# Pacing the late input loads of a fused attention and MoE kernel by the stage two units ahead

## The chip, the cores and the metric

The kernel runs on one core of a Trainium2 chip. The metric is the device time of one execution in microseconds (us); the median of several runs is compared. Engines are named as the profile names them: PE is TensorE (PEld its weight loads), DVE is VectorE, ACT is ScalarE, POOL is GpSimd and SP is SyncE, whose only work here is to issue DMAs.

## What is computed

The reference is causal attention followed by one gated two-layer block, here called the MoE as the program calls it. Four batches, 8 heads, 768 positions, head size 64. Heads 0, 2 and 6 see all earlier positions; the five others see the first 4 positions and a window of 64.

```python
scores = scale * np.matmul(q, k.transpose(0, 1, 3, 2))
mask = np.where(retr, causal, causal & (is_sink | in_win))
a = softmax(np.where(mask, scores, -1e9))
x = (a @ v).transpose(0, 2, 1, 3).reshape(B * S, H * D)     # 3072 x 512
h = x @ w_in                                                # 512 -> 2048
out = (h * sigmoid(beta * h)) @ w_out                       # 2048 -> 512
```

## The kernel before, in words

The 3072 rows are cut into 8 **units** of 384 rows: unit n is half u = n % 2 of batch b = n // 2. A unit goes through these stages, and the units overlap.

- **Loads.** Units 0 to 3 load q and k in pairs of heads. Units 4 to 7 (`n >= TD`) load whole blocks: `load_block` (line 307) issues three DMAs of 256 KB for q and three for k, `load_v` (line 331) three for v, all from SP, into a ring `wf` of three buffers.
- **Turning q and k.** For units 4 to 7 POOL casts the blocks to bf16 tiles `c` (`cast_block`), and `turn_block` (line 324) has three DMA transposes, issued from SP, write them into the tile `QK`. All three must have landed before the unit's scores.
- **Scores.** PE multiplies QK into PSUM tiles `sp` (two in the ring, used by PV as well), ACT takes exponentials into `es`, DVE masks them.
- **Sums and spread.** `sums` (line 540) sums `es` on PE, `recips_d` takes the reciprocal on DVE into `rec`. For units 4 to 7 `spread_w` (line 565) writes it to DRAM as `rd` with three small DMAs and `spread_r` (line 570) reads it back as `R`, repeated over 64 partitions, with two DMAs. All are issued from SP. Units 0 to 3 spread it on PE instead.
- **PV and norm.** `pv` (line 604) multiplies `es` with v into two `sp` tiles; `norm` (line 632) multiplies those by `R` on DVE into `xT` and frees the `sp` tiles.
- **MoE.** 16 steps of `mm1` (four matmuls of xT with w_in), tanh on ACT into `t`, the gate on DVE into `gT`, and 48 matmuls of gT with w_out in `mm2`, taken in threes. Copies to `osb` and one store to `out` for each 128 rows, issued from SP.

The order of all instructions is written by a planner, `_Plan` (line 50). Each operation is entered with a priority, an engine, a cost, what it needs and what it gives, and the rings it takes from; `run` walks through time and writes one list for each engine. The costs, `needs` and `gives` act in the planner alone. On the chip an engine goes through its list in order, and an instruction waits for the data and buffers that it touches, and for nothing else. So an entry in `needs` that names no data of the instruction decides its place in the list and makes no wait.

Of the kernel before, what the change touches and what calls it, by code (L numbers as in the profile page):

```python
# [49 lines left out]
class _Plan:  # L50
# [9 lines left out]
    def add(self, key, eng, cost, f, needs=(), gives=(), take=(), drop=(), dma=0.0, mode=None, port=False, begun=()):  # L60

        one = isinstance(eng, str)
        alts = [(eng, cost)] if one else list(zip(eng, cost))
        self.ops.append((key, len(self.ops), dict(alts), (lambda e: f()) if one else f, tuple(needs), tuple(gives),
                         tuple(take), tuple(drop), dma, mode, port, tuple(begun)))
# [76 lines left out]
def kernel(  # L142
# [14 lines left out]
    pe, dve, act, pool, sp = (_Ordered(tc, e) for e in (nc.tensor, nc.vector, nc.scalar, nc.gpsimd, nc.sync))  # L157
    B, H, S, D = q.shape
    d_model, d_ff = moe_w_in.shape
    FO = d_ff // 128  # L160
    NP = len(PAIRS)
# [4 lines left out]
    def tpool(name, bufs, space=None):  # L166
# [5 lines left out]
        sp=2, b=4, **{f"es{pi}_{u}": 1 for pi in range(NP) for u in range(2)})  # L172
# [45 lines left out]
    NS = 8  # L218
# [342 lines left out]
    def recips_d(x):  # L561
        x.rec = rp.tile([96, 128], F32, name="rec")
        dve.reciprocal(x.rec, x.sm[0:96, 0:128])

    def spread_w(x):
        x.rd = dp.tile([8, TU, 128], F32, name="rd")
        for j in range(TU):
            sp.dma_start(out=x.rd[:, j, :], in_=x.rec[32 * j:32 * j + 8, :])

    def spread_r(x):  # L570
        x.R = rp.tile([128, NP, NQ], F32, name="R", bufs=RINGS["R"])
        src = x.rd[:]
        for i in range(2):
            sp.dma_start(
                out=x.R[i * D:(i + 1) * D],
                in_=bass.AP(src.tensor, src.offset + i * NQ, [[0, D], [2 * NQ, NP], [1, NQ]]))

    def recips(x):
        dve.reciprocal(x.sm[0:96, 0:128], x.sm[0:96, 0:128])

    def split(x):
        hi = rp.tile([96, 128], BF16, name="hi")
        rec = x.sm[0:96, 0:128]
        dve.tensor_copy(out=hi, in_=rec)
        for j in range(TU):
            r = slice(32 * j, 32 * j + 32)
            dve.scalar_tensor_tensor(out=hl[r, j * 128:(j + 1) * 128], in0=hi[r], scalar=low[r], in1=rec[r],
                                     op0=MULT, op1=ADD)

    def spread(x, t):  # L590
        if t == 0:
            x.R = rp.tile([128, NP, NQ], F32, name="R", bufs=RINGS["R"])
        ps = bank((x.n, "R", t))
        pe.matmul(ps[:, 0:NQ], sel[0:96, 2 * t:2 * t + 2, :].rearrange("p a d -> p (a d)"), hl[0:96, :],
                  start=True, stop=True)
        x.ps["R", t] = ps

    def spread_copy(x, t, eng):
        cast(eng, x.R[:, t, :], x.ps.pop(("R", t))[:, 0:NQ])
# [80 lines left out]
    add = plan.add  # L680
    ENG = {"act": act, "dve": dve, "pool": pool, "sp": sp}

    def attention(n, key, early):
        x = units[n]
        b, u = x.b, x.u
        gate = [("begun", "o", NS // 2 - 1)] if b else []

        for pi in range(NP if n < TD else 0):
            for nm in ("q2", "k2"):
                e = "act" if n == 0 and nm == "k2" else "sp"  # L690
                add(key["lq"] + 0.01 * pi, e, 0.47, lambda pi=pi, nm=nm, e=e: load_qk(x, pi, nm, ENG[e]), dma=0.64, needs=gate,
                    gives=[("f", n, pi, nm)], take=[(nm + "f", (n, pi), 1)])
# [3 lines left out]
                    needs=[("f", n, pi, nm)] + ([("begun", n, pi)] if nm == "k2" else []), gives=[("c", n, pi, nm)],  # L696
                    begun=[("begun", n, pi)] if nm == "q2" else [],
                    take=[("c", (n, pi), 1)] if nm == "q2" else [], drop=[(nm + "f", (n, pi))])
        if n >= TD:
            for i in range(2):  # L700
                add(key["lq"] + 0.1 * i, "sp", 3.0, lambda i=i: load_block(x, i), dma=3.9, needs=gate,
                    gives=[("f", n, i)], take=[("wf", (n, "b", i), TU)])
                for j in range(TU):
                    add(key["T"][0] - 2 + 0.5 * j + 0.1 * i, "pool", 0.7, lambda i=i, j=j: cast_block(x, i, j, pool),
                        needs=[("f", n, i)] + ([("c", n, 0, j)] if i else []), gives=[("c", n, i, j)],
                        take=[("c", (n, j), 1)] if i == 0 else [], drop=[("wf", (n, "b", i))])
            for j in range(TU):
                add(key["T"][0] + 0.5 * j, "sp", 1.25, lambda j=j: turn_block(x, j), dma=0.7,
                    needs=[("c", n, 0, j), ("c", n, 1, j)] + [("sc", n - 4 + v, pi) for pi in range(NP) for v in range(2 - u) if n >= 4],
                    gives=[("QKb", n, j)], drop=[("c", (n, j))])  # L710
            add(key["T"][0] + 1.5, "pool", 0.02, lambda: None, needs=[("QKb", n, j) for j in range(TU)],
                gives=[("QK", n, pi, i) for pi in range(NP) for i in range(2)])
        for j in range(TU):
            if not b:
                add(key["lv"] + 0.01 * j, "sp", 1.0, lambda j=j: load_v(x, j, sp), dma=1.3,
                    gives=[("vf", n, j)], take=[("vf", (n, j), 1)])
            elif j == 0:
                add(key["lv"], "sp", 3.0, lambda: [load_v(x, j, sp) for j in range(TU)], dma=3.9, needs=gate,
                    gives=[("vf", n, j) for j in range(TU)], take=[("wf", (n, 0), TU)])
            add(key["cv"] + 0.5 * j, "pool", 0.58, lambda j=j: cast_v(x, j, pool),  # L720
                needs=[("vf", n, j)] + ([("v", n - u, 0)] if (u, j) != (0, 0) else []),
                gives=[("v", n, j)], drop=[("wf" if b else "vf", (n, 0 if b else j))], take=[("vb", b, 5)] if (u, j) == (0, 0) else [])
        add(key["cv"] + 2, ("dve", "pool") if n else ("pool",), (0.9, 1.8), lambda e: shift_v(x, ENG[e]), port=True,
            needs=[("v", n, j) for j in range(TU)] + ([("v", n - 1, TU - 1)] if u else []), gives=[("vs", n)], take=[("vs", n, 2)])
# [9 lines left out]
        for pi in range(NP if n < TD else 0):  # L734
# [3 lines left out]
                gives=[("T", n, pi)], take=[("b", (n, "T", pi), 2 if early else 1)], drop=[("c", (n, pi))])  # L738
            if early:
                for i in range(2):  # L740
                    add(k0 + 0.1, ("act", "dve"), (0.37, 0.465), lambda e, pi=pi, i=i: qk_copy(x, pi, ENG[e], i, 1),
                        needs=[("T", n, pi)] + wait, gives=[("QK", n, pi, i)], drop=[("b", (n, "T", pi))])
            else:
                add(k0 + 0.1, ("act", "dve"), (0.7, 0.87), lambda e, pi=pi: qk_copy(x, pi, ENG[e]),
                    needs=[("T", n, pi)] + wait, gives=[("QK", n, pi, 0), ("QK", n, pi, 1)], drop=[("b", (n, "T", pi))])
        for pi in range(1, NP):
            if not u:
                k0 = key["T"][pi]
                add(k0 + 0.2, ("pool", "dve"), (0.35, 0.3), lambda e, pi=pi: ks_copy(x, pi, ENG[e]), port=True,
                    needs=[("QK", n, pi, 1), ("const", "zero")] + ([("sc", n - 4 + j, 3) for j in range(2)] if n >= 4 else []),  # L750
                    gives=[("KS", n, pi)])
# [3 lines left out]
        for bi, bu in enumerate(bursts):  # L755
            k0 = key["B"][bi] if not early else key["T"][bu[0][0]] + 0.5 + 0.2 * bu[0][1]
            needs, take, gives, drop, cost = [], [], [], [], 0.1
            for (pi, ri) in bu:
# [14 lines left out]
                needs=needs, gives=gives, take=take, drop=drop, mode="qk")  # L773
            for j, (pi, ri) in enumerate(bu):
                half = rounds_of(pi, u)[ri][1] is None
                add(k0 + 0.1 + 0.02 * j, "act", 0.38 if half else 0.7, lambda pi=pi, ri=ri: exps(x, pi, ri),
                    needs=[("S", n, pi, ri)], gives=[("E", n, pi, ri)], drop=[("sp", (n, pi, ri))])
                c = mask_cost(pi, ri, u)
                if c:
                    add(k0 + 0.2 + 0.02 * j, "dve", c, lambda pi=pi, ri=ri: masks(x, pi, ri, dve), port=True,  # L780
                        needs=[("E", n, pi, ri), ("const", "mask", u)], gives=[("M", n, pi, ri)])
# [4 lines left out]
        if n < RD:  # L786
            add(key["S"] + 0.1, "dve", 0.88, lambda: recips(x), needs=[("sum", n)], gives=[("rec", n)])
            add(key["S"] + 0.2, "dve", 1.3, lambda: split(x), needs=[("rec", n), ("const", "sel"), ("const", "zero")], gives=[("hl", n)],
                take=[("hl", n, NP)], drop=[("b", (n, "s"))])
            for t in range(NP):  # L790
                add(key["S"] + 0.3 + 0.01 * t, "pe", 0.18, lambda t=t: spread(x, t),
                    needs=[("hl", n)] + ([("sb", n, 0)] if t else []), gives=[("sb", n, t)],
                    take=[("b", (n, "R", t), 1)] + ([("R", n, 2)] if t == 0 else []), drop=[("hl", n)])
                add(key["S"] + 0.4, ("act", "dve"), (0.37, 0.465), lambda e, t=t: spread_copy(x, t, ENG[e]),
                    needs=[("sb", n, t)], gives=[("R", n, t)], drop=[("b", (n, "R", t))])
        else:
            add(key["S"] + 0.1, "dve", 1.0, lambda: recips_d(x), needs=[("sum", n)], gives=[("rec", n)],
                take=[("rec", n, 1)], drop=[("b", (n, "s"))])
            add(key["S"] + 0.2, "sp", 1.4, lambda: spread_w(x), needs=[("rec", n)], gives=[("rd", n)], dma=0.1, drop=[("rec", n)])
            add(key["S"] + 0.3, "sp", 0.9, lambda: spread_r(x), needs=[("rd", n)], gives=[("R", n, t) for t in range(NP)], dma=2.3,  # L800
                take=[("R", n, 2)])
        for g in range(2):
            drop = [(f"es{pi}_{u}", n) for pi in [(0, 1, 3), (2, 3)][g]] + [("vb", b), ("vs", n), ("VK", b)]
            add(key["PV"][g], "pe", [[0.65, 0.65], [1.2, 1.2]][u][g], lambda g=g: pv(x, g),
                needs=M + vready + [("rec", n) if n < RD else ("R", n, 0)], gives=[("o", n, g)], take=[("sp", (n, "v", g), 1)], drop=drop, mode="pv")
            add(key["PV"][g] + 0.1, "dve", 0.87, lambda g=g: norm(x, g),
                needs=[("R", n, 2 * g), ("R", n, 2 * g + 1), ("o", n, g)] + ([("xT", n, 0)] if g else []),
                gives=[("xT", n, 2 * g), ("xT", n, 2 * g + 1)],
# [32 lines left out]
    for n in range(N):  # L841
        u = n % 2
        if n == 0:
            attention(n, dict(lq=-100, lv=-99.5, cv=-97.5, T=[-98, -97, -96, -95], S=-94, PV=[-93.9, -93.8]), True)
        elif n == 1:
            attention(n, dict(lq=-99.4, lv=-99.05, cv=-90, T=[-90, -89, -88, -87], S=-80, PV=[-79.9, -79.8]), True)
        else:
            base = 16 * (n - 1)
            key = dict(lq=base - 34, lv=base - 32, cv=base - 20, T=[base - t for t in (25.5, 24.5, 23.5, 22.5)],
                       B=[base - t for t in ([18, 16, 14], [20, 18, 16, 14, 12, 11])[u]], S=base - 9.5,  # L850
                       PV=[base - 4.5, base - 3.5])
            attention(n, key, None)
# [4 lines left out]
        needs=[("beta_p",)], gives=[("beta",)], drop=[("b", "beta")])  # L857
# [8 lines left out]
    for s in range(NS // 2):  # L866
        for w, k0, ld, ca in (("i", -99.2 + 0.2 * (s // 2), load_w_in, cast_w_in), ("o", -98.3, load_w_out, cast_w_out)):
            add(k0 + 0.01 * s, "sp", 1.3 if w == "i" else 0.65, lambda s=s, ld=ld: ld(s), dma=3.15, gives=[("wf", w, s)], begun=[("begun", w, s)],
                take=[("wf", (w, s), 4)])
            for i in range(4):  # L870
                add(k0 + 0.01 * s, "pool", 0.58, lambda s=s, i=i, ca=ca: ca(s, i, pool), needs=[("wf", w, s)],
                    gives=[("w" + w, 4 * s + i)], drop=[("wf", (w, s))])
# [42 lines left out]
```

## Time and profile before

| What | Value |
|---|---|
| median of 3 runs | 263.28 us (263.11 to 263.43) |
| the profiled execution's own time | 261.98 us |
| its span in the trace | 260.3 us |
| PE busy | 234.9 us, 90% of the span |
| DVE, ACT, POOL busy | 58%, 56%, 28% |
| bytes over DMA | 40.27 MB, mean 155 GB/s |
| mean granted PE clock | 0.98 |

The busy shares say which engine has the most work. The page's row of 40 slices says where in the span it rests, and the views by engine and by wait say what it rests for. Times in all views count from the start of the span.

### The profile page before, as it was taken

The numbers are of one execution on the slowest core, as the hardware profiler recorded it, in microseconds if no ns is written. First come the engines' busy times: TensorE is split into PE (matmuls) and PEld (weight loads), VectorE is DVE, ScalarE is ACT, GpSimd is POOL, SyncE is SP. The second block draws the span as 40 slices with busy tenths as digits, with TensorE's granted clock in tenths as the row PEclk, the third lists the DMA queues.
The fourth block names the chain that finished last, engine by engine and source line by source line (L and its number), as shares of the span: only waits on it lengthen the run. The fifth ranks groups of instructions, "written<-read, shape, count | busy, mean of one in ns | idle before, by whom it ended". The sixth has DMA issues, their size and how long they took to land.

```text
span 260.3 us, 5563 instructions
## 1 busy us (share of the span) xinstructions
PE 234.9 (90%) x2167; PEld 128.5 (49%) x2193; DVE 150.3 (58%) x316; ACT 146.0 (56%) x248; POOL 73.9 (28%) x159
## 2 busy tenths in 40 slices
PE   1768999999999999999980999999999999999994
PEld 1435456664555555455440455645554465555541
DVE  5777789879556666656324364585465554454400
ACT  2666985788559662853831474285358734445410
POOL 5463848856983443442500000000000000000000
PEclk9999999999999999999996599999999999999999
DMA  6999998998999999999995012410251016101122
GB/s 191 273 301 305 205 317 307 341 253 189 237 230 210 238 203 194 237 209 210 227 194 123 0 43 65 100 40 0 83 122 44 1 46 161 42 0 40 43 81 81
DMA packets 81531, 40.27 MB, mean 155 GB/s; under 512 B 63984, under 2 KB 74336, under 8 KB 81504
## 3 DMA queue, kind: packets, MB, share of 16 engines
q1 hardware_dynamic: 80384, 39.12, 64.6%
q10 hardware_dynamic: 1120, 0.79, 1.1%
q8 instruction: 17, 0.28, 0.4%
q14 instruction: 10, 0.08, 0.1%
HBM read 30.42 MB, written 6.34 MB: 141 GB/s over the span
## 4 chain that ended last, share of the span: by engine, by line
PE 70%; DMA 11%; DVE 6%; ACT 5%; issue 3%; SPq 3%; POOL 1%; POOLq 0%; DVEq 0%; ACTq 0%
PE b L44 59%; PE sp L44 11%; DMA wf<-in_v_dram 4%; DMA k2f<-in_k_dram 3%; SPq L44 3%; ACT es L44 2%; DMA R<-rd 2%; ACT t L44 1%; DVE QK L44 1%; DVE es L44 1%; DVE vs L44 1%; DMA QK<-c 1%; DVE xT L44 1%; DVE gT L44 1%; POOL vb L44 0%
## 5 line engine op out<-in xcount | busy, mean ns | idle before, releaser
L44 ACT ACTIVATE t<-b,beta_h 128x384 f32<-128x384 f32 x128 | 73.0, 586 | 63.1 <-PE b L44 58.7
L44 PE MATMUL b<-xT,w_in 128*128 128x384 bf16 x512 | 101.3, 331 | 0.3
L44 DVE SCALAR_TENSOR_TENSOR gT<-t,b 128x384 bf16<-128x384 f32 x128 | 69.2, 553 | 48.5 <-ACT t L44 47.5
L44 PE MATMUL b<-w_out,gT 128*128 128x512 bf16 x358 | 94.0, 379 | 2.1 <-issue 1.3
L44 PEld LDWEIGHTS <-w_in 128*128 128x128 bf16 x512 | 48.5, 99 | 42.4 <-issue 5.6
L44 ACT ACTIVATE es<-sp 128x768 bf16<-128x768 f32 (+1 forms) x68 | 50.9, 798 | 22.2 <-PE sp L44 22.0
L44 PEld LDWEIGHTS <-gT 128*128 128x128 bf16 x384 | 36.4, 98 | 34.6 <-issue 0.8
L44 PE MATMUL sp<-QK 64*64 64x128 bf16 (+5 forms) x368 | 23.9, 259 | 10.9 <-DVE xT L44 8.5
L44 POOL CAST c<-wf 128x256 bf16<-128x256 f32 x48 | 18.3, 416 | 23.6 <-DMA QK<-c 10.0
L44 PEld LDWEIGHTS <-QK 64*64 64x64 bf16 (+1 forms) x368 | 11.2, 110 | 27.5 <-issue 20.0
L44 DVE TENSOR_TENSOR xT<-sp,R 128x768 bf16<-128x768 f32 x16 | 15.1, 956 | 10.5 <-DMA R<-rd 7.9
L44 DVE TENSOR_TENSOR es<-es,mask_s 128x768 bf16<-128x768 bf16 (+1 forms) x24 | 15.2, 647 | 6.1 <-ACT es L44 5.3
L44 ACT ACTIVATE osb<-b 128x512 f32<-128x512 f32 x18 | 10.7, 595 | 12.1 <-PE b L44 11.9
L44 DVE TENSOR_TENSOR es<-es,mask_c 128x256 bf16<-128x256 bf16 (+2 forms) x32 | 9.8, 321 | 11.5 <-ACT es L44 11.1
L44 PE MATMUL sp<-es,vb 128*64 128x64 bf16 (+3 forms) x228 | 16.0, 242 | 0.0
L44 POOL CAST vb<-wf 128x512 bf16<-128x512 f32 x18 | 11.1, 618 | 8.4 <-DMA wf<-in_v_dram 8.1
L44 ACT COPY QK<-b 128x384 bf16<-128x384 bf16 (+1 forms) x14 | 8.2, 599 | 8.5 <-PE b L44 7.3
L44 POOL CAST w_in<-wf 128x512 bf16<-128x512 f32 x16 | 9.7, 650 | 11.0 <-DMA wf<-in_moe_w_in_dram 11.0
L44 PEld LDWEIGHTS <-vb 128*64 128x64 bf16 x228 | 11.9, 111 | 1.4
L44 PE MATMUL b<-ident,c 128*128 128x128 bf16 x96 | 9.9, 253 | 1.9 <-ACT c L44 0.9
L44 PE MATMUL sp<-es,vs 128*64 128x64 bf16 x120 | 10.9, 196 | 0.0
L44 PE MATMUL b<-es,esel 128*32 128x128 bf16 x372 | 10.7, 227 | 0.0
(68 smaller groups left out, 147.8 us busy)
## 6 DMA issues: line engine op xcount, KB each, us to landing
out_dram<-osb SPq DMA_DIRECT2D x24, 256.0 KB, 4.1
wf<-in_v_dram SPq DMA_DIRECT2D x18, 256.0 KB, 5.4
wf<-in_moe_w_out_dram SPq DMA_DIRECT2D x4, 1024.0 KB
q2f<-in_q_dram SPq DMA_DIRECT2D x16, 192.0 KB, 4.8
wf<-in_moe_w_in_dram SPq DMA_DIRECT2D x4, 768.0 KB, 8.6
wf<-in_q_dram SPq DMA_DIRECT2D x12, 256.0 KB, 4.6
wf<-in_k_dram SPq DMA_DIRECT2D x12, 256.0 KB, 4.2
R<-rd SPq DMA_DIRECT2D x8, 384.0 KB, 5.1
```

What stands on the lines that cost most here:

```text
L44: ins = f(*a, **k)
```

## The change

Two places in `attention` are edited.

```diff
-        gate = [("begun", "o", NS // 2 - 1)] if b else []
+        gate = ([("begun", "o", NS // 2 - 1)] if b else []) + ([("h", n - 2, 0)] if n > 3 else [])
...
-            add(key["S"] + 0.3, "sp", 0.9, lambda: spread_r(x), needs=[("rd", n)], gives=[("R", n, t) for t in range(NP)], dma=2.3,
+            add(key["S"] + 0.3, "sp", 0.9, lambda: spread_r(x), needs=[("rd", n)], gives=[("R", n, t) for t in range(NP)], dma=4.0,
```

`gate` stands in the `needs` of the q, k and v loads. With the new entry the planner places the loads of unit n (4 to 7) only after the first MoE step of unit n - 2. The second edit has the planner expect `R` 1.7 later. Both change the lists of all engines behind them; the set of instructions stays the same, but for a few copies that change engine.

On SP, around the spread of unit 4: in the list of before the loads of unit 7 (`in_k`, `in_v`) and a store stand ahead of `rd`, and the transposes of unit 7 between `rd` and `R`. The second `rd` and `R` are those of unit 5.

```order
L44 DMA wf<-in_k_dram 128x8x64 x3
L44 DMA wf<-in_v_dram 128x8x64 x3
L44 DMA out_dram<-osb 128x512
L44 DMA rd<-rec 8x128 x3
L44 DMA_TRANSPOSE QK_107<-c 128x8x128 x3
L44 DMA out_dram<-osb 128x512
L44 DMA R<-rd 64x4x384 x2
L44 DMA out_dram<-osb 128x512 x2
L44 DMA rd<-rec 8x128 x3
L44 DMA R<-rd 64x4x384 x2
```

The same place in the list of the change. The loads and the transposes here are those of unit 5, and the loads of unit 6 follow behind `R` and two stores.

```order
L44 DMA wf<-in_q_dram 128x8x64 x3
L44 DMA wf<-in_k_dram 128x8x64 x3
L44 DMA wf<-in_v_dram 128x8x64 x3
L44 DMA out_dram<-osb 128x512
L44 DMA rd<-rec 8x128 x3
L44 DMA_TRANSPOSE QK_106<-c 128x8x128 x3
L44 DMA R<-rd 64x4x384 x2
L44 DMA out_dram<-osb 128x512 x2
L44 DMA wf<-in_q_dram 128x8x64 x3
L44 DMA wf<-in_k_dram 128x8x64 x3
L44 DMA wf<-in_v_dram 128x8x64 x3
```

The pattern nine loads, a store, `rd`, three transposes of the next unit, `R` now comes three times, for units 4, 5 and 6. Before, all loads and transposes stood ahead of the first `R`.

On DVE, around the reciprocal of unit 4, before (`KS` are small copies of keys, here of unit 6; `QK_107` is its QK tile):

```order
L44 TENSOR_SCALAR osb<-b_2033 128x512
L44 SCALAR_TENSOR_TENSOR gT<-t,b_2126 128x384
L44 COPY KS_111<-QK_107 64x4 x2
L44 COPY KS_112<-QK_107 64x4 x2
L44 SCALAR_TENSOR_TENSOR gT<-t,b_2140 128x384
L44 RECIPROCAL rec<-b_2150 96x128
L44 SCALAR_TENSOR_TENSOR gT<-t,b_2199 128x384
```

and in the list of the change:

```order
L44 TENSOR_SCALAR osb<-b_1964 128x512
L44 SCALAR_TENSOR_TENSOR gT<-t,b_2053 128x384
L44 SCALAR_TENSOR_TENSOR gT<-t,b_2073 128x384
L44 RECIPROCAL rec<-b_2079 96x128
L44 SCALAR_TENSOR_TENSOR gT<-t,b_2124 128x384
```

The four copies are gone from ahead of the reciprocal, since unit 6 has not been loaded yet at that point. On PE the list stays the same up to the first scores of unit 5, which now stand three MoE steps later (a first-layer, a second-layer and a first-layer step), and the first scores of units 6 and 7 stand 14 and 15 MoE steps behind the sums of units 5 and 6.

## Rows read from the trace of the kernel before

**Rows 1.** The page: busy time by engine, and the granted clock in 40 slices.

```profile
PE 234.9 (90%) x2167; PEld 128.5 (49%) x2193; DVE 150.3 (58%) x316; ACT 146.0 (56%) x248; POOL 73.9 (28%) x159
...
PEclk9999999999999999999996599999999999999999
```

**Rows 2.** One stretch of 4 us: busy time by engine, granted clock, DMA share, GB/s.

```profile
144.00:148.00 4.00, 4.00 (x21) 1.70 (x20) 1.67 (x3) 1.97 (x3) 0.00 (x0) 0.50 0.00 0
```

**Rows 3.** Waits from 130 to 150 us: engine, releaser, total, times, longest.

```profile
DVE xT L44 <- DMA R<-rd: 7.9, 1, 7.9
PE sp L44 <- DVE xT L44: 7.0, 2, 5.4
```

**Rows 4.** The chain that ended last: start, us, what.

```profile
134.15 6.15 DMA R<-rd
...
148.02 1.10 PE sp L44 x18
```

**Rows 5.** SP's issues in order of time: start, us, operation.

```profile
113.78 2.16 SPq L44 DMA_TRANSPOSE QK<-c  x1
...
119.55 2.52 SPq L44 DMA_DIRECT2D wf<-in_k_dram  x3
122.17 3.65 SPq L44 DMA_DIRECT2D wf<-in_v_dram  x3
...
127.48 1.01 SPq L44 DMA_DIRECT2D rd<-rec  x3
128.60 4.02 SPq L44 DMA_TRANSPOSE QK<-c  x3
...
133.43 1.58 SPq L44 DMA_DIRECT2D R<-rd  x2
```

**Rows 6.** DVE in order of time, in brackets the idle time before and its releaser.

```profile
118.27 1.07 DVE L44 COPY KS<-QK 64x4 bf16<-64x4 bf16 x4 [0.70 <-DMA QK<-c]
...
119.85 0.95 DVE L44 RECIPROCAL rec<-b 96x128 f32<-96x128 f32 x1
```

**Rows 7.** PE in order of time, around the sums of unit 4 and the stop.

```profile
117.46 0.95 PE L44 MATMUL b<-es,esel 128*32 128x128 bf16 x32
...
125.59 0.50 PE L44 MATMUL sp<-QK 64*128 64x384 bf16 x4
...
132.81 3.19 PE L44 MATMUL b<-w_out,gT 128*128 128x512 bf16 x14 [0.16 <-issue]
141.44 0.50 PE L44 MATMUL sp<-QK 64*128 64x256 bf16 x4 [5.44 <-DVE xT L44]
143.53 0.54 PE L44 MATMUL sp<-QK 64*64 64x64 bf16 x14 [1.59 <-DVE xT L44]
144.00 4.02 PE L44 MATMUL b<-xT,w_in 128*128 128x384 bf16 x12
```

**Rows 8.** PE in order of time, the same steps two units later.

```profile
198.31 0.63 PE L44 MATMUL sp<-QK 64*128 64x256 bf16 x18
198.87 1.47 PE L44 MATMUL b<-xT,w_in 128*128 128x384 bf16 x8
...
200.92 0.91 PE L44 MATMUL sp<-QK 64*64 64x64 bf16 x22
201.77 0.82 PE L44 MATMUL b<-xT,w_in 128*128 128x384 bf16 x4
202.43 0.81 PE L44 MATMUL b<-w_out,gT 128*128 128x512 bf16 x3
```

**Rows 9.** POOL in order of time: a cast that waits for a transpose to free its buffer.

```profile
118.39 0.75 POOL L44 CAST c<-wf 128x256 bf16<-128x256 f32 x2 [2.31 <-DMA QK<-c]
```

**Rows 10.** ACT in order of time: the last output copy of unit 1.

```profile
107.30 0.60 ACT L44 ACTIVATE osb<-b 128x512 f32<-128x512 f32 x1
```

**Rows 11.** Time from issue to landing, all in us: tiles QK, then wf, then R.

```profile
DMA to landing us min/median/max: 4.8/4.8/4.8
...
DMA to landing us min/median/max: 3.6/4.4/7.2
...
DMA to landing us min/median/max: 4.5/5.1/5.9
```

## The prediction

> **What bounds the kernel now.** I began with the page: TensorE is busy in 90% of the span and nothing else comes near it, so a change pays where it takes away rest of TensorE. The row of 40 slices shows the granted clock at full speed except in two slices, about 137 to 150 us, in [rows 1]. The reader should then look at 4 us windows around that place: from 144 to 148 the clock is at half, 1.2 instead of 2.4 GHz, though TensorE is busy throughout [rows 2]. The waits from 130 to 150 say what came before it: DVE waited 7.9 us for the transfer into `R`, and TensorE 7.0 us in two pieces, the longer of 5.4, for the `xT` that DVE makes of it [rows 3]. The chain that ended last runs through that transfer, 134.15 to 140.30 [rows 4]. So there is one stop, and it belongs to the spread of unit 4.
>
> Why was `R` late? The sums of unit 4 ended at 118.41 [rows 7] and the reciprocal at 120.80 [rows 6]. SP then still issued loads of unit 7 up to 125.8 and a store; the write `rd` came at 127.48, the transposes of unit 7 at 128.60, `R` at 133.43 [rows 5]. That is 12.6 us between the reciprocal and the issue of `R`, of which `rd` itself took 1.0. SP issued things that nobody needed yet.
>
> **What the stop costs.** Second-layer matmuls ended at 136.00 (132.81 and 3.19) [rows 7], and work at full clock went on after the 22 scores that end at 149.12 [rows 4]: 13.12 us. In between stand 18 scores, 12 first-layer matmuls and 22 scores. Two units later the same groups show what they take: 18 scores 0.56 (198.31 to 198.87), 22 scores 0.85 (200.92 to 201.77), four first-layer matmuls 0.66 (201.77 to 202.43), so twelve 1.98 [rows 8]; together 3.39. The stop costs 13.12 - 3.39 = **9.7 us**. Of this 7.03 is waiting (5.44 and 1.59) [rows 7] and 2.7 the low clock behind it: 12 first-layer matmuls in 4.02 instead of 1.98, the rest in the scores.
>
> **What the change removes.** In the new SP list only the nine loads and the transposes of unit 5 stand around the spread of unit 4. The new entry in `gate` is no wait on the chip, so no engine holds SP up for it: the loads go out behind the last store of unit 1, whose copy ends at 107.90 [rows 10]. Three loads took 2.52 to 3.65 [rows 5], so the keys are issued by 115.2 and all nine by 118.9; landing took 4.4 as a median and 7.2 at most [rows 11], so the last key block is there by 119.6 to 122.4 and cast 0.75 later [rows 9]. This lies beside MoE work of TensorE.
>
> Then the steps, from the end of the sums at 118.41. The reciprocal took 0.95 and stood behind four small copies (1.07) which are gone; with a gate operation ahead of it I take 1.2 to its end, 119.6; the bounds are 1.0 and the 2.4 of before [rows 6, 7]. `rd` 1.0, three transposes 4.0, gaps 0.2: SP is at 124.8 [rows 5]. Two issues of `R`, the second some 0.8 later, and 6.15 from there to landing, as in [rows 4], give `R` at 131.8. TensorE has 12 second-layer matmuls ready behind its PV products (12/14 of 3.19, from 132.8) and needs the first `xT` at 135.5, `R` therefore at 134.5, a norm of about 1 us earlier. That leaves 2.7 us. Thus the stop of 9.7 goes, and with it the low clock.
>
> **What the change adds.** The keys of unit 5 were there long before; now their transposes are issued behind `rd`, so behind the sums of unit 4, and what is late next is `QK`. Behind the waiting scores TensorE holds all else in its list, the MoE of unit 3 too. From the issue of a transpose to landing the trace has 4.8 [rows 11], some 3.5 after its issue ends when three take 4.0; the cast that waited for one began 2.45 after it (115.94 to 118.39) [rows 5, 9]. I take 2.5, since that row is a waiting instruction's own start, and keep 3.5 as the bound. So `QK` is ready 1.2 + 1.0 + 4.0 + 0.2 + 2.5 = 8.9 us after the sums. TensorE asked for these scores at 125.59 before [rows 7] and now three steps of 0.66 later [rows 8], at 127.6: 9.2 after the sums. For units 6 and 7 the 14 and 15 steps behind the sums give 9.2 and 9.9. The margins are 0.3, 0.3 and 1.0: nearly nothing for two units. At the other end, 2.4 for the reciprocal, 1.0, 4.0, 0.2 and 3.5 make 11.1, a wait of 1.9, 1.9 and 1.2, together 5.0. I take 0.7 for the three units, near the low end, because the row with three transposes right behind `rd` is the row of before with the same neighbours [rows 5].
>
> The other edits cost nothing. The larger planned time for `R` only moves PV products in the list, by steps that fill the place. The loads of units 5 to 7 now run beside MoE work to about 180 us; the matmuls there read no tile that they write. Unit 4 is loaded some 15 us later, but its scores came late enough: I leave it without a price, up to 1 us. POOL's casts move later with the loads, and POOL is busy in 28% of the span [rows 1].
>
> **The sum.** The profiled execution took 261.98: 261.98 - 9.7 + 0.7 = 253.0. The median of the runs is 1.3 above that execution (263.28), which I carry over: **254.3 us**.
>
> A rule that speaks against it: DMA: Bandwidth & Descriptors, section Issuing engines are not separate DMA queues, of the Trainium skill says that what a sequencer spends on starting a DMA is usually small beside the transfer, and that transfers from all queues share the same engines. By that rule the order of SP would hardly matter and only thinner traffic would help. Here the trace disagrees: 12.6 us before the issue, 6.9 after it.
>
> **The rivals.**
>
> *Keys late by a little.* The bound above: waits of 5.0 in three units instead of 0.7. For it: margins of 0.3. Against it: 2.45 in the row that shows it. 261.98 - 9.7 + 5.0 + 1.3 = 258.6, still faster.
>
> *The stop stays.* `R` still stands behind three transposes, and if its lateness came from the traffic of the loads, only its landing shortens, from 6.15 to the median of 5.1 [rows 4, 11]: 263.28 - 1.05 = 262.2. Against it stands the issue at 133.43. This is the time that the rule above would give.
>
> *Slower: the keys set the pace.* Loads one unit ahead leave each unit's scores hanging on a chain of reciprocal, `rd`, transposes and landing. If `QK` comes 3 us late for units 5, 6 and 7 and the clock falls each time as it did (2.7), this costs 3 x 5.7 = 17.1: 261.98 - 9.7 + 17.1 + 1.3 = 270.7. It decides from 3.2 us for each unit with the clock counted in (9.7 / 3), so from 0.5 of wait where the clock falls, from 3.2 where it doesn't. Against it: the upper bound of the chain is 11.1, a wait of 1.9, and TensorE fell to half only within a wait of 5.4. The Trainium skill takes this side: its front page, Trainium Kernel Development and Optimization, section Best Practices, wants double buffering so that transfers lie beside computing, and the change gives up most of that lead. No run here shows yet what the smaller lead costs.
>
> **How the numbers follow.** The forecast has 0.75, keys late by a little 0.13, the stop stays 0.05, slower 0.07. Low end of the range: no new waits and runs like the profiled one, 261.98 - 9.7 = 252.3. High end: the first rival, 258.6. That holds about 8 in 10, since the forecast and the first rival, with 0.88, may miss by something that I have not seen. A measurement of this kernel tells 0.2% (0.5 us) from no change. Faster by more: the forecast, the first rival and 0.03 of the second, 0.91. Within 0.2%: 0.02. Slower by more: 0.07.
>
> **What would show it right or wrong.** In the profile of the changed kernel the slices should have no low clock between the start and the end, and TensorE no wait over 2 us for `xT` after 44 us. `R` for unit 4 should be issued near 125 us instead of 133.43, right behind the transposes of unit 5. The waits of the first scores of units 5, 6 and 7 for `QK` should be under 1 us each. The span should end near 251.3. The prediction is wrong if a wait for `xT` of several us stands behind the PV products of unit 4, 5 or 6, or if those first scores wait long enough that the clock falls.

## The result and the profile after

The changed kernel takes 252.76 us as a median (251.96 to 253.78, 4 runs), the kernel before beside it 263.19 (262.71 to 263.43, 4 runs): a ratio of 0.9608, 95% interval 0.9569 to 0.9647. **Faster by 3.9%.** The profiled execution took 252.49 us, with a span of 250.8 where before had 260.3. Runs in the chip's second, slower state are left out of every median here and below.

The page of the changed kernel, the rows that answer to [rows 1]: busy time, and the granted clock in 40 slices.

```profile
PE 234.8 (94%) x2193; PEld 127.7 (51%) x2193; DVE 149.2 (59%) x318; ACT 145.4 (58%) x249; POOL 72.6 (29%) x156
...
PEclk9999999999999999999999999999999999999999
```

The span is 9.5 shorter, and the dip of the clock in [rows 1] is gone. That TensorE's busy time is nearly the same is a coincidence: the 234.9 of before hold some 2.7 of matmuls at the low clock, and that trace lists 2167 matmuls where this one lists 2193, so short gaps stand in it for some work. SP in order of time around the spread of unit 4, and then of unit 5 (start, us, operation); [rows 5] before:

```profile
110.50 3.40 SPq L44 DMA_DIRECT2D wf<-in_k_dram  x3
114.00 3.69 SPq L44 DMA_DIRECT2D wf<-in_v_dram  x3
117.79 1.09 SPq L44 DMA_DIRECT2D out_dram<-osb  x1
119.75 1.01 SPq L44 DMA_DIRECT2D rd<-rec  x3
120.87 4.01 SPq L44 DMA_TRANSPOSE QK<-c  x3
125.05 1.32 SPq L44 DMA_DIRECT2D R<-rd  x2
...
148.02 0.97 SPq L44 DMA_DIRECT2D rd<-rec  x3
149.10 4.04 SPq L44 DMA_TRANSPOSE QK<-c  x3
```

`R` is issued at 125.05 and not at 133.43. DVE in order of time answers to [rows 6] and to the wait of 7.9 in [rows 3]:

```profile
118.78 0.94 DVE L44 RECIPROCAL rec<-b 96x128 f32<-96x128 f32 x1
...
132.96 0.95 DVE L44 TENSOR_TENSOR xT<-sp,R 128x768 bf16<-128x768 f32 x1
133.83 0.54 DVE L44 SCALAR_TENSOR_TENSOR gT<-t,b 128x384 bf16<-128x384 f32 x1
134.29 0.95 DVE L44 TENSOR_TENSOR xT<-sp,R 128x768 bf16<-128x768 f32 x1
```

Neither norm has a bracket: no wait for `R` is left. TensorE, as in [rows 7]:

```profile
117.66 0.95 PE L44 MATMUL b<-es,esel 128*32 128x128 bf16 x32
...
127.73 0.50 PE L44 MATMUL sp<-QK 64*128 64x384 bf16 x4
...
133.42 2.76 PE L44 MATMUL b<-w_out,gT 128*128 128x512 bf16 x12
136.12 0.63 PE L44 MATMUL sp<-QK 64*128 64x256 bf16 x18
136.68 2.12 PE L44 MATMUL b<-xT,w_in 128*128 128x384 bf16 x12
138.73 0.91 PE L44 MATMUL sp<-QK 64*64 64x64 bf16 x22
139.58 0.82 PE L44 MATMUL b<-w_out,gT 128*128 128x512 bf16 x3
```

The 18 scores, 12 first-layer matmuls and 22 scores that stood between 136.00 and 149.12 now stand between 136.12 and 139.58: 3.46 us instead of 13.12. That is 9.66, and the span is 9.5 shorter: the whole gain in the span lies in this one place. The sums end at 118.61 and ended at 118.41, so nothing was won ahead of it. Nothing was lost elsewhere: between 60 and 250 us the trace lists no wait of TensorE, so none of the first scores of units 5, 6 and 7 either. Between the medians the difference is 10.4; the 0.8 beyond the stretch is less than executions of this one kernel differ by (251.96 to 253.78).

### The profile page after: what moved, and what is told of

Same layout as the page of the kernel before. It is cut to its first block, busy times and chain, and to the rows that moved or that the text cites. A ratio compares the mean times of both kernels' runs of the same rounds, so it can differ in the third digit from the quotient of the medians.

```text
span 250.8 us, 5576 instructions
## 1 busy us (share of the span) xinstructions
PE 234.8 (94%) x2193; PEld 127.7 (51%) x2193; DVE 149.2 (59%) x318; ACT 145.4 (58%) x249; POOL 72.6 (29%) x156
## 4 chain that ended last, share of the span: by engine, by line
PE 86%; ACT 4%; DVE 4%; DMA 3%; issue 1%; ACTq 0%
PE b L44 73%; PE sp L44 13%; DMA k2f<-in_k_dram 3%; ACT es L44 2%; DVE QK L44 1%; ACT t L44 1%; DVE es L44 1%; DVE R L44 0%; DVE xT L44 0%; ACT osb L44 0%; DVE gT L44 0%; ACT R L44 0%; DVE KS L44 0%; ACT QK L44 0%; ACT c L44 0%
## 5 line engine op out<-in xcount | busy, mean ns | idle before, releaser
L44 PE MATMUL b<-w_out,gT 128*128 128x512 bf16 x384 | 98.8, 380 | 0.0
L44 PE MATMUL b<-xT,w_in 128*128 128x384 bf16 x512 | 98.2, 327 | 0.1
L44 PE MATMUL sp<-QK 64*64 64x128 bf16 (+5 forms) x368 | 23.3, 252 | 3.9 <-DVE QK L44 1.6
```

The costliest lines, as they stand in the source:

```text
L44: ins = f(*a, **k)
```

## Experiments

Each kernel was compared with the kernel before on the same chip. The first four ask what made the stop, the others how near the change lies to a new one.

### The planned time of `R` alone

```diff
-lambda: spread_r(x), needs=[("rd", n)], ..., dma=2.3,
+lambda: spread_r(x), needs=[("rd", n)], ..., dma=4.0,
```

> The planned time of R alone (2.3 to 4.0), loads as in the kernel before. Its SP list keeps all loads and transposes ahead of the first R. Queue theory (R was late because SP issued it late): the stop stays, R of unit 4 issued near 133 us, time 263.2 us, within 0.5. Traffic theory (R was late because the loads shared the DMA engines with it): the same, 263.2. If the planned time of R did the work: about 253.

Measured: 261.75 us, ratio 0.9962 (0.993 to 0.9994). The stop stays. TensorE and DVE in order of time, only rows with waits:

```profile
143.20 0.48 PE L44 MATMUL b<-xT,w_in 128*128 128x384 bf16 x2 [4.30 <-DVE xT L44]
145.29 2.08 PE L44 MATMUL b<-xT,w_in 128*128 128x384 bf16 x6 [1.60 <-DVE xT L44]
```

```profile
142.19 0.96 DVE L44 TENSOR_TENSOR xT<-sp,R 128x768 bf16<-128x768 f32 x1 [6.70 <-DMA R<-rd]
```

The planner put a little more work ahead of the norm, so 5.9 us of waiting are left of 7.03. `R` is as late as before. By itself this edit is worth 0.4% (0.1 to 0.7).

### The gate alone

```diff
-gate = [("begun", "o", NS // 2 - 1)] if b else []
+gate = ([("begun", "o", NS // 2 - 1)] if b else []) + ([("h", n - 2, 0)] if n > 3 else [])
```

> The gate alone, R planned as before (2.3). SP list as in the change, but two of the three transposes of unit 6 stand ahead of the rd of unit 5. Queue theory: R of unit 4 issued near 125 us, no wait over 1 us, 252.8 us within 0.8. Traffic theory: the same 252.8. If both edits are needed: between 255 and 263.

Measured: 253.96 us, ratio 0.9675 (0.9627 to 0.9722), span 251.0. The gate does it. SP's issue of `R`, and the row of DVE that tells when `R` came:

```profile
124.81 1.32 SPq L44 DMA_DIRECT2D R<-rd  x2
```

```profile
131.72 1.82 DVE L44 TENSOR_TENSOR xT<-sp,R 128x768 bf16<-128x768 f32 x2 [1.08 <-DMA R<-rd]
```

Here `R` was issued at 124.81, and the norm that waited for it began 6.9 later. In the changed kernel that makes 125.05 + 6.9 = 131.95, one us ahead of the first norm at 132.96.

To see if the second edit adds anything, the changed kernel was run again on the chip of the last three experiments:

> The changed kernel once more, word for word, beside the others on one chip. 252.8 us. Beside it stands the kernel with the gate alone (253.96, ratio 0.9675), whose lists differ by the planned time of R: if that edit is worth nothing, the ratio here lies within 0.967 +- 0.005; if it is worth the 1.2 us between the medians, at 0.961.

Measured: 253.16 us (251.94 to 253.59), ratio 0.9667 (0.962 to 0.9714), span 251.7. It lies on the ratio of the gate alone. The two intervals overlap nearly in full, so these runs show no gain of the second edit on top of the gate. The 0.9608 of the result and this 0.9667 are one kernel on two occasions; the difference is what such a comparison leaves open.

### Only the loads of unit 7 held back

The kernel before with the gate for `n > 6` alone; the planned time of `R` as before.

> The gate for unit 7 alone, R planned as before. Loads of units 4 to 6 run ahead as early as in the kernel before; the last two transposes of unit 6 and a store stand ahead of the rd of unit 4, and R comes right behind it. Queue theory: R of unit 4 issued near 123 us, no stop, 252.8 us within 0.8. Pacing theory (each unit must be held back, as the change does): the stop shrinks only in part, 256 to 262.

Measured: 254.07 us, ratio 0.967 (0.9611 to 0.973), span 252.3. SP in order of time:

```profile
118.13 0.36 SPq L44 DMA_DIRECT2D out_dram<-osb  x1
120.55 1.01 SPq L44 DMA_DIRECT2D rd<-rec  x3
122.63 1.32 SPq L44 DMA_DIRECT2D R<-rd  x2
```

Units 4 to 6 are loaded as early as before, and the time is that of the gate alone. So it is the last unit's loads and transposes, and no others, whose place ahead of `rd` and `R` made the stop. TensorE's longest wait for `xT` is 0.5. In the changed kernel three transposes still stand between `rd` and `R` and TensorE has no wait, so transposes there are not enough by themselves; the loads of unit 7 without its transposes were not run.

### Queue or traffic: `rd` and `R` issued by ACT

The kernel before, with all its loads where they were; only the engine that issues the spread differs.

```diff
-            sp.dma_start(out=x.rd[:, j, :], in_=x.rec[32 * j:32 * j + 8, :])
+            act.dma_start(out=x.rd[:, j, :], in_=x.rec[32 * j:32 * j + 8, :])
...
-            sp.dma_start(
+            act.dma_start(
...
-            add(key["S"] + 0.2, "sp", 1.4, lambda: spread_w(x), ...
-            add(key["S"] + 0.3, "sp", 0.9, lambda: spread_r(x), ...
+            add(key["S"] + 0.2, "act", 1.4, lambda: spread_w(x), ...
+            add(key["S"] + 0.3, "act", 0.9, lambda: spread_r(x), ...
```

> Loads, transposes and their order on SP as in the kernel before, but rd and R of units 4 to 7 issued from ACT instead of SP. Queue theory: R of unit 4 is issued within 4 us of the reciprocal (near 124 us), the stop of 9.7 us goes; ACT loses some us to issuing and to waiting for rd, so 253 to 256 us. Traffic theory: the loads of unit 7 share the DMA engines with R as before, R lands near 138 to 140 and the stop stays, 261 to 264 us.

Measured: 254.24 us (253.08 to 254.44), ratio 0.9681 (0.9628 to 0.9734), span 252.5. ACT, SP and DVE in order of time:

```profile
120.74 1.22 ACTq L44 DMA_DIRECT2D rd<-rec  x3
122.05 1.14 ACT L44 ACTIVATE t<-b,beta_h 128x384 f32<-128x384 f32 x2 [1.46 <-DMA rd<-rec]
...
125.74 1.47 ACTq L44 DMA_DIRECT2D R<-rd  x2
```

```profile
119.41 2.65 SPq L44 DMA_DIRECT2D wf<-in_k_dram  x3
122.16 3.87 SPq L44 DMA_DIRECT2D wf<-in_v_dram  x3
126.12 1.27 SPq L44 DMA_DIRECT2D out_dram<-osb  x1
127.50 8.34 SPq L44 DMA_TRANSPOSE QK<-c  x3
```

```profile
134.64 0.96 DVE L44 TENSOR_TENSOR xT<-sp,R 128x768 bf16<-128x768 f32 x1 [2.00 <-DMA R<-rd]
```

The loads of unit 7 go out at 119.41 and 122.16, within 0.2 us of [rows 5], and yet the stop is gone. So the loads and transposes did their harm by their place in SP's list, and not by the bytes. What runs beside `R` has a price too: the norm begins 8.9 after the first issue of `R` (125.74 to 134.64) and not 6.9 as with the gate alone, and TensorE waits 1.32 for `xT`. Whether the loads, the slow transposes or the other issuing engine cost these 2 us was not told apart. The transposes took 8.34 here, beside a DMA share of 1.21, and 4.02 before, behind the same loads [rows 5], beside 1.03; `R` in flight is what is new beside them. ACT pays with 1.46 of idle time, in which it issues the three writes of `rd` (1.22). None of this is a stop like that of before.

### How much room the keys have

The changed kernel, with small DMAs that nobody reads on SP ahead of the transposes of units 5, 6 and 7: six, then twelve. No list differs otherwise.

```diff
+    pad = consts.tile([FO, 18, 8], F32, name="pad")
...
     def turn_block(x, j):
+        if j == 0 and 2 * x.b + x.u > 4:
+            for i in range(6):
+                sp.dma_start(out=pad[:, (2 * x.b + x.u - 5) * 6 + i, :], in_=moe_beta.rearrange("(fo fi) -> fo fi", fi=128)[:, 0:8])
```

> The changed kernel, with six small DMAs (16 rows of 32 bytes, read by nobody) that SP issues right ahead of the three key transposes of units 5, 6 and 7; every list of instructions is otherwise the same. At 0.34 us each (three writes of rd take 1.01) they put the transposes some 2.1 us later. It tells how much room the keys have. By the margins of the prediction (0.3, 0.3 and 1.0 us) the first scores of the three units wait 1.8, 1.8 and 1.1: together 4.7, 257.2 us. By what the changed kernel shows (transposes end at 124.88, 153.14 and 180.17, first scores at 127.73, 156.12 and 183.67, and one landing 3.3 us after the start of the transpose that it belongs to, so some 1.2 after its end) the margins are 1.6, 1.8 and 2.3, and the waits 0.5, 0.3 and 0: 253.5 us. If keys never set a time: 252.7.

> The same with twelve such DMAs, some 4.1 us. By the margins of the prediction: waits of 3.8, 3.8 and 3.1 in the three units, 10.7 us, so 263.4; with the low clock behind each wait (2.7 each time, as before the change) 271.5. By the margins read from the changed kernel (1.6, 1.8, 2.3): 2.5, 2.3 and 1.8, together 6.6, so 259.3 without a fall of the clock and up to 267 with one behind each. R, issued 4.1 later, at 129.2, lands at 135 to 136, 2 to 3 us after the norm takes it in the changed kernel, but the norm itself comes later by the wait for the keys, so no wait for R over 1 us. In any case this tells how a chain of rd, transposes and landing that is too long is paid for.

Measured with six: 259.46 us, ratio 0.9922 (0.9887 to 0.9956). With twelve: 272.62 us (270.72 to 274.15), ratio 1.0412 (1.0345 to 1.0479), **slower than before**. With six, SP and TensorE in order of time, the latter at the first scores of units 5, 6 and 7:

```profile
119.59 1.01 SPq L44 DMA_DIRECT2D rd<-rec  x3
120.65 3.40 SPq L44 DMA_DIRECT2D pad<-in_moe_beta_dram  x6
124.15 4.01 SPq L44 DMA_TRANSPOSE QK<-c  x3
...
152.05 0.97 SPq L44 DMA_DIRECT2D rd<-rec  x3
153.07 2.64 SPq L44 DMA_DIRECT2D pad<-in_moe_beta_dram  x6
155.81 4.03 SPq L44 DMA_TRANSPOSE QK<-c  x3
```

```profile
130.18 0.50 PE L44 MATMUL sp<-QK 64*128 64x384 bf16 x4 [2.55 <-DMA QK<-c]
...
161.78 0.51 PE L44 MATMUL sp<-QK 64*128 64x384 bf16 x6 [1.56 <-DMA QK<-c]
...
190.92 0.50 PE L44 MATMUL sp<-QK 64*128 64x384 bf16 x4 [1.51 <-DMA QK<-c]
```

and with twelve:

```profile
132.55 0.82 PE L44 MATMUL sp<-QK 64*128 64x384 bf16 x4 [4.92 <-DMA QK<-c]
...
168.20 0.82 PE L44 MATMUL sp<-QK 64*128 64x384 bf16 x6 [4.33 <-DMA QK<-c]
...
201.87 0.82 PE L44 MATMUL sp<-QK 64*128 64x384 bf16 x4 [3.83 <-DMA QK<-c]
```

The small DMAs took more than the 0.34 each that was expected, so the shift is read from the rows. In unit 5 the transposes start 4.56 after `rd` (119.59 to 124.15), in the changed kernel 1.12: 3.44 later. TensorE waits 2.55 of it, so the margin was 0.89. The same working gives 1.12 for unit 6 and 1.37 for unit 7, and from the twelve 0.82, 1.14 and 1.62. Room for the keys: **0.9, 1.1 and 1.5 us**.

Neither set of margins in the expectations was right. The larger one came from a slip. The landing is counted from the start of a transpose, and the last one takes 1.29, so its 3.3 end 2.0 after the issues, and not 1.2. The waiting scores confirm it: they start 1.9 to 2.1 after the third transpose has been issued, in all six places (128.16 to 130.18 in unit 5 with six).

The spans show what a wait costs beyond itself. With six, 258.2 - 250.8 = 7.4, of which 5.62 is waiting. With twelve, 271.5 - 250.8 = 20.7, of which 13.08 is waiting. The rest, 1.8 and 7.6, is nearly all low clock, as the same matmuls show. From the first scores of unit 5 to a group of 18 scores behind them the changed kernel takes 8.39 (127.73 to 136.12). That group with six, then with twelve:

```profile
140.16 0.63 PE L44 MATMUL sp<-QK 64*128 64x256 bf16 x18
...
143.81 0.63 PE L44 MATMUL sp<-QK 64*128 64x256 bf16 x18
```

So the stretch takes 9.98 with six (from 130.18) and 11.26 with twelve (from 132.55): 1.6 more behind the wait of 2.55, 2.9 more behind 4.92. Measured in the same way, the two later waits with six cost nothing beyond themselves, and those with twelve 2.2 (behind 4.33) and 2.4 (behind 3.83). Stretches with six, then with twelve: from and to, length, busy time of PE, PEld, DVE, ACT, POOL, granted clock, DMA share, GB/s.

```profile
128.00:132.00 4.00, 1.82 (x10) 0.81 (x11) 0.55 (x1) 1.69 (x3) 0.00 (x0) 0.93 0.84 179
132.00:136.00 4.00, 4.00 (x16) 1.24 (x14) 0.56 (x1) 2.33 (x5) 0.00 (x0) 0.64 0.58 152
...
158.00:164.00 6.00, 4.44 (x28) 2.20 (x27) 3.61 (x13) 3.00 (x5) 0.00 (x0) 1.00 0.88 182
```

```profile
132.00:136.00 4.00, 3.45 (x12) 1.36 (x13) 0.00 (x0) 1.51 (x2) 0.00 (x0) 0.50 0.92 220
...
164.00:172.00 8.00, 3.80 (x15) 1.66 (x16) 2.00 (x8) 2.09 (x3) 0.00 (x0) 0.63 0.94 207
...
198.00:204.00 6.00, 2.17 (x9) 0.72 (x9) 0.82 (x2) 2.09 (x3) 0.00 (x0) 0.68 0.92 208
```

With six, the clock fell behind the wait of 2.55 and stayed at 1.00 around the two of some 1.5. With twelve, it fell behind all three. The stop of before cost 2.7 in this way, behind 5.44 and 1.59. The fall behind 2.55 may not be the same each time: in five of the twelve executions with six the mean clock of the whole run was 0.997 or 0.998, and 0.993 in the profiled one. With six one norm waits 0.47 for `R`, with twelve none; TensorE has no wait for `xT` in either.

### Loads four steps later

```diff
-... + ([("h", n - 2, 0)] if n > 3 else [])
+... + ([("h", n - 2, 4)] if n > 3 else [])
```

> The changed kernel with the gate four first-layer steps later, at the fifth step of the MoE two units ahead and not at its first. The planner then moves work too. Its own list has TensorE idle for some 4.6 us in all between 60 and 225 us, nearly all of it in the last two units, where the changed kernel's has 0.2. If loads take on the chip what is planned: some 4 us slower, 257. If the room read from the changed kernel (1.6 us or more for each unit) takes a part: 254 to 255. If the place of the gate does not matter as long as it lies behind the spread: 252.7, like the changed kernel.

Measured: 256.10 us, ratio 0.9772 (0.9717 to 0.9827), span 254.4: 2.9 us over the changed kernel on the same chip (253.16), between the answers of the planner's list (257) and of the room for the keys (254 to 255). Two stretches of this kernel:

```profile
136.00:200.00 64.00, 63.04 (x594) 33.44 (x592) 33.79 (x67) 36.24 (x59) 13.02 (x30) 1.00 0.76 165
200.00:225.00 25.00, 23.43 (x274) 13.68 (x267) 14.23 (x26) 14.19 (x24) 0.00 (x0) 1.00 0.18 44
```

TensorE is idle for 2.5 us in these 89, where the changed kernel has none; the planner's list had 4.6 between 60 and 225. No wait is longer than 1.0, none of them is for a DMA (they are for ACT and DVE), and the clock stays up there. So in this kernel the place of the gate cost time through the order that the planner wrote, though no transfer was late.

## Why the prediction was right

The forecast was 254.3 us (252.3 to 258.6), 0.91 for faster; measured 252.76. By its own steps:

- **What the stop costs, 9.7.** The stretch went from 13.12 to 3.46, and the span from 260.3 to 250.8. The two parts, waiting and the low clock behind it, went together, as in the prediction.
- **Why `R` was late: SP issued other things first.** Shown from three sides: with the same loads and another issuing engine the stop goes; with the loads of unit 7 alone held back it goes; with a longer planned time alone it stays. The rule on issuing engines from the Trainium skill (DMA: Bandwidth & Descriptors, section Issuing engines are not separate DMA queues) would, as the prediction took it, have kept the time near 262.2. The prediction set the 12.6 us ahead of the issue against this rule, but the rule is on starting one DMA, and those 12.6 us were a dozen issues in one list; one issue of `R` took 0.8 against a landing of 6.15, which agrees with the rule. Its part on shared transfer engines would fit the 2.0 us that `R` takes longer with the loads beside it (8.9 against 6.9), though no run shows that it is the reason, and moving the issue to another engine gave nearly the whole gain (ratio 0.9681).
- **The steps to `R`.** Reciprocal done at 119.72 (119.6 predicted), SP at 124.88 behind the transposes (124.8), `R` issued at 125.05 ("near 125"). From its first issue to landing it took 6.9 in the kernel with the gate alone (7.0 predicted); in the changed kernel nothing waits for `R`, so no row shows when it landed.
- **New waits of 0.7 for the keys: the term that was mis-sized.** It is 0. The chain from the sums to `QK` was taken as 8.9, of which 2.5 was landing behind the last transpose; the waiting scores show 1.9 to 2.1. So the margins are 0.9, 1.1 and 1.5 instead of 0.3, 0.3 and 1.0, and nothing waits. The 2.5 came from a transpose in another place [rows 9]: its issue alone took 2.16 [rows 5], where the last one here takes 1.29, and the DMA share around it was 1.25 and not 0.86. DVE was released there at 118.27 [rows 6], close to POOL's 118.39, so the landing itself was near 2.4 in that place and is 2.0 in this one. And the 0.7 is no sum: margins of 0.3 give no wait, the upper bound gives 5.0, and 0.7 was chosen between them.
- **The offset of 1.3** between the profiled execution and the median was carried over. In the changed kernel it is 0.27 (252.49 and 252.76). The sum itself, 261.98 - 9.7, gives 252.3 for the profiled execution against 252.49. These two terms, 0.7 and 1.0 too much, less the 0.2, make up the 1.5 us between forecast and median.
- **The slower rival, keys that set the pace.** It did not come true, but its mechanism is real and near: with 5.4 to 5.7 us more ahead of the transposes the kernel takes 272.62, against 270.7 that the rival was given. The point at which it decides, a mean of 3.2 for each unit with the clock counted in, lies between the two kernels: six small DMAs cost 7.4 in all and twelve 20.7. The prediction reckoned with a fall of the clock behind a wait of 0.5; in the profiled execution the waits of some 1.5 did not bring it down.

The Trainium skill's front page (Trainium Kernel Development and Optimization, section Best Practices) asks for double buffering, so that DMA overlaps compute. The changed kernel still has that: from 136 to 200 us TensorE is busy throughout, beside a DMA share of 0.73. What it gave up is lead. The runs bound this: the lead could be cut to what leaves the keys 0.9 us, since the list that it emptied was worth 9.7, while delays of 2.7 to 3.4 us more gave 6.3 back (259.46 against 253.16 on the same chip).

## What to carry to other kernels

A prefetch costs more than bandwidth when it shares an in-order issuing queue with a small transfer that is on the critical path: compare the time from ready to issue with the time from issue to landing, and if the first is the longer, change the order, the issuing engine or the pace. Hold back only what stands in front; here one unit of four was enough. Then measure the room that is left by adding a known delay, because a trace without a wait doesn't show how near the next one is.

## What the runs showed of the hardware

- Where the clock fell, a wait cost TensorE 1.6 to 2.9 us beyond itself: 1.6 behind 2.55, 2.2 to 2.9 behind waits of 3.83 to 5.44. Around the waits of 1.5 no fall was seen.
- Three DMA transposes took SP 4.0 us to issue both beside a DMA share of 0.72 (changed kernel, from 149.10) and beside 1.03 (before, from 128.60), and 8.34 beside 1.21 (`R` issued by ACT, from 127.50). A single one took 2.16 beside 1.25 (before, from 113.78).
- A DMA of 16 rows of 32 bytes held SP for 0.44 to 0.57 us, more than one of the `rd` writes (0.34), though it moves less.
